# An attention stage whose tile pairs share transposes, with half-sums moved by DMA and operand moves issued a tile later

## The chip, the core and the metric

The kernel runs on one core of a Trainium2 chip. The metric is the device time of one execution in microseconds (us). Engines are named as in the profile: PE is the matmul engine, PEld its weight load, DVE, ACT and POOL the three elementwise engines, SP the engine that issues most of the DMAs.

## The reference

Attention with a bucket mask, then two mixture-of-experts layers on its output. Only the attention stage is changed:

```
q_bits = (einsum('bhsd,dk->bhsk', q, proj) > 0)          # 6 bits give a bucket; k_bits alike
mask   = q_bucket[:, :, :, None] == k_bucket[:, :, None, :]
scores = where(mask, q @ k.T / sqrt(D), -1e9)
scores = scores - max(scores, -1)
attn   = exp(scores);  attn = attn / (sum(attn, -1) + 1e-9)
out    = attn @ v                                         # B=2, H=8, S=768, D=64
x      = out as (1536, 512);  then _moe_ref(x), then _moe2_ref
```

## The kernel before

The 16 heads are worked on as 8 **head pairs** (n). A head pair has 12 **tiles** (t), six for each of its two heads (s), of 128 query rows by 768 keys; 96 tiles in all. A tile's place in its pair is called **r** here (0 to 11). fp32 products are made of a high and a low part (`hi`, `lo`, `ah`, `al`), each of which the PE multiplies at full rate.

A tile goes through these steps, each a function: `qk` (PE: four matmuls into the PSUM tile S, of which there are two), `soft` (DVE: row maximum), `expo` (ACT: exponential and row sum), `inv` (DVE: two small instructions that invert the sum), `norm` (POOL: 128x768 times that inverse), `tr` (PE: six 128x128 transposes into PSUM tiles `tp`, of which there are three), `trh` and `trl` (ACT and DVE: high and low part of the transposed tile, into `ah` and `al`), `av` (PE: matmuls of `ah` and `al` with the V operand `vv` into O). After two tiles, O holds a finished **unit** of 256 query rows: `xa` (ACT) copies it out, and `xp` (POOL, three instructions, only for the second head) adds the two halves and splits the result into the two parts of X, which the expert layer reads.

Beside this, tiles r = 0 to 9 prepare the next head pair in steps `pp`, `pa`, `pd` (function `prep`): r = 0 to 3 transpose raw q and k (`rq`, `rk`), r = 4 and 5 compute the bucket bits (`prep_bits`, six matmuls each), r = 6 to 9 expand them (`prep_hot`). The finished operands are moved by SP's DMAs (`stack`) into the tiles `qa, ka, qb, kb` that `qk` reads. At r = 11 `load` fetches raw q, k and v of the head pair after the next; its `rq` is first read one tile later, at r = 0.

The order of the work is written out by hand: for each tile the loop goes through a table of (step, lag) and calls the step for tile t - lag. There is one table for most tiles, and others for the first and the last head pair, by t's parity. Each engine, and SP's queue too, executes what the loop emits in that order, so that an instruction that waits holds up all that stands behind it on its engine.

After the attention stage comes `_moe_ref`: PE forms the gate's scores from X (lines 476 and 477), weights are fetched in pieces `raw` (three buffers), split by ACT and DVE (lines 427 and 428) into `big`, and PE's first expert products (line 563, `hp`) begin.

Of the kernel before, what the change touches and what calls it, by code (L numbers as in the profile page):

```python
# [39 lines left out]
}  # L40
PREP_V = (3, 3, 6, 9)
# [14 lines left out]
def kernel(ctx, tc, q, k, v, proj, wg1, w1, w2, wg2, w1b, w2b, out):  # L56
    nc = tc.nc
# [224 lines left out]
    def soft(t):  # L282
        w = ap.tile([128, 4], F32, name="w", bufs=6)
        nc.vector.tensor_reduce(w[:, 0:1], Sp[t % 2], op=OP.max, axis=AX.X, negate=True)  # L284
        EN[t] = w

    def expo(t):
        w = EN[t]
        e = ap.tile([128, S], F32, name="e", bufs=2)
        nc.scalar.activation(e, Sp[t % 2], AF.Exp, bias=w[:, 0:1], scale=1.0, accum_out=w[:, 1:2])  # L290
        EN[t] = (e, w)

    def inv(t):
        e, w = EN[t]
        nc.vector.tensor_scalar(w[:, 2:3], w[:, 1:2], 1e-9, None, op0=OP.add)
        nc.vector.reciprocal(w[:, 3:4], w[:, 2:3])  # L296

    def norm(t):
        e, w = EN[t]
        a = ap.tile([128, S], F32, name="a", bufs=3)  # L300
        nc.gpsimd.tensor_tensor(a, e, w[:, 3:4].to_broadcast([128, S]), op=OP.mult)  # L301
        EN[t] = a

    def tr(t, c):
        u, i = divmod(t, 2)
        if i == 0 and c == 0:
            AT[u] = (ap.tile([128, R, 2, 128], F32R, name="ah", bufs=2),
                     ap.tile([128, R, 2, 128], F32R, name="al", bufs=2))
# [5 lines left out]
    def trh(t, c):  # L314
        u, i = divmod(t, 2)
        nc.scalar.activation(AT[u][0][:, 3 * c:3 * c + 3, i, :], TP[t, c], AF.Copy)  # L316

    def trl(t, c):
        u, i = divmod(t, 2)
        ah, al = AT[u]  # L320
        nc.vector.tensor_tensor(al[:, 3 * c:3 * c + 3, i, :], TP[t, c], rd(ah[:, 3 * c:3 * c + 3, i, :]), op=OP.subtract)  # L321


    def av(t):
        u, c = divmod(t, 2)
# [41 lines left out]
    def ahead_v(t):  # L367
# [845 lines left out]
```

## Time and profile before

| | us |
|---|---|
| median of 3 runs (1584.17 to 1585.69) | 1584.64 |
| the profiled execution, its own time | 1586.3 |
| its span in the trace | 1584.6 |
| PE busy in the span | 1553.6 (98%) |
| first score matmul to last one started | 13.64 to 258.04 |

The span is what the trace covers; the profiled execution's time is 1.7 us longer. A matmul's length in the trace covers its whole passage through the array, and matmuls overlap, so the distance from one start to the next is what a matmul costs in a row of them; the same holds, to a smaller degree, of ACT and DVE. "Idle before" in brackets is the time that the engine stood idle ahead of the instruction, with what ended it.

### The profile page before, as it was taken

The numbers are of one execution on the slowest core, as the hardware profiler recorded it, in microseconds if no ns is written. First come the engines' busy times: TensorE is split into PE (matmuls) and PEld (weight loads), VectorE is DVE, ScalarE is ACT, GpSimd is POOL, SyncE is SP. The second block draws the span as 40 slices with busy tenths as digits, with TensorE's granted clock in tenths as the row PEclk, the third lists the DMA queues.
The fourth block names the chain that finished last, engine by engine and source line by source line (L and its number), as shares of the span: only waits on it lengthen the run. The fifth ranks groups of instructions, "written<-read, shape, count | busy, mean of one in ns | idle before, by whom it ended". The sixth has DMA issues, their size and how long they took to land.

```text
span 1584.6 us, 21591 instructions
## 1 busy us (share of the span) xinstructions
PE 1553.6 (98%) x8482; PEld 1309.4 (83%) x8482; DVE 813.0 (51%) x1977; ACT 472.0 (30%) x951; POOL 270.7 (17%) x313
## 2 busy tenths in 40 slices
PE   8999998999999999999999999999999999999998
PEld 6888887788888888888888888888887767888998
DVE  6998897612423324333333332134676377667533
ACT  6998997212200211221221121021121210011343
POOL 4888887020000000000000000000000000111221
PEclk9999999999999999999999999999999999999999
DMA  8665560120200110110120020011000116545531
GB/s 190 147 146 138 121 160 27 42 93 19 77 12 14 67 41 3 64 54 1 38 83 0 14 80 27 1 54 53 1 14 14 41 41 221 190 175 190 190 137 31
DMA packets 83542, 119.13 MB, mean 75 GB/s; under 512 B 43184, under 2 KB 46256, under 8 KB 83440
## 3 DMA queue, kind: packets, MB, share of 16 engines
q1 hardware_dynamic: 75920, 105.15, 22.4%
q0 software_dynamic: 2176, 6.29, 1.3%
q10 hardware_dynamic: 5344, 6.30, 1.1%
q8 instruction: 67, 1.10, 0.3%
q14 instruction: 35, 0.29, 0.1%
HBM read 83.91 MB, written 9.44 MB: 59 GB/s over the span
## 4 chain that ended last, share of the span: by engine, by line
PE 89%; ACT 3%; DVE 3%; DMA 1%; POOL 1%; issue 1%; SPq 1%; POOLq 0%; ACTq 0%; DVEq 0%
PE hp L563 33%; PE yp L582 29%; PE hp L940 5%; PE yp L884 4%; PE tp L311 3%; PE O L331 3%; PE yp L993 3%; PE S L280 2%; PE yp L996 1%; PE sp L1077 1%; PE tp L202 1%; ACT e L290 1%; ACT ah L316 1%; PE yp L998 1%; PE tp L173 1%
## 5 line engine op out<-in xcount | busy, mean ns | idle before, releaser
L563 PE MATMUL hp<-X,big 128*128 128x512 f32 x2304 | 528.9, 390 | 0.0
L563 PEld LDWEIGHTS hp<-X,big 128*128 128x128 f32 x2304 | 431.7, 188 | 89.9
L582 PE MATMUL yp<-big 128*128 128x512 f32 x2016 | 461.2, 389 | 0.0
L582 PEld LDWEIGHTS yp<-big 128*128 128x128 f32 x2016 | 378.2, 188 | 78.4
L564 ACT ACTIVATE big<-hp 128x512 fp32r<-128x512 f32 x176 | 105.2, 598 | 757.5 <-PE hp L563 757.1
L565 DVE SCALAR_TENSOR_TENSOR big<-hp,big 128x512 fp32r<-128x512 f32 x176 | 121.7, 691 | 252.5 <-ACT big L564 252.5
L587 DVE SCALAR_TENSOR_TENSOR acc<-yp,P,acc 128x512 f32<-128x512 f32 x72 | 54.1, 751 | 258.4 <-PE yp L582 258.4
L865 POOL DMA_INDIRECT raw<-x2h,who x4 | 4.1, 1026 | 949.5 <-DVE wg2b L1062 939.0
L301 POOL TENSOR_TENSOR a<-e,w 128x768 f32<-128x768 f32 x96 | 140.8, 1469 | 45.9 <-DVE w L296 26.1
L321 DVE TENSOR_TENSOR al<-tp,ah 128x384 fp32r<-128x384 f32 x192 | 102.8, 547 | 19.1 <-ACT ah L316 18.7
L311 PE MATMUL tp<-ident,a 128*128 128x128 f32 x576 | 94.4, 276 | 8.4 <-ACT hot L233 2.7
L316 ACT ACTIVATE ah<-tp 128x384 fp32r<-128x384 f32 x192 | 91.1, 488 | 16.4 <-PE tp L311 15.9
L940 PE MATMUL hp<-raw,big 128*128 128x192 f32 x488 | 93.7, 338 | 1.2 <-ACT raw L918 1.2
L284 DVE TENSOR_REDUCE w<-S 128x1 f32<-128x768 f32 x96 | 91.1, 949 | 5.1 <-PE S L280 5.1
L311 PEld LDWEIGHTS tp<-ident,a 128*128 128x128 f32 x576 | 67.1, 140 | 24.8 <-issue 5.8
L290 ACT ACTIVATE e<-S,w 128x768 f32<-128x768 f32 x96 | 86.6, 902 | 0.7 <-POOL a L301 0.6
L428 DVE TENSOR_TENSOR big<-raw,big 128x1024 fp32r<-128x1024 f32 x63 | 76.6, 1221 | 14.5 <-ACT big L427 11.1
L940 PEld LDWEIGHTS hp<-raw,big 128*128 128x128 f32 x488 | 79.7, 193 | 2.7 <-ACT raw L918 1.6
L331 PE MATMUL O<-ah,vv 128*128 128x256 f32 x288 | 80.6, 309 | 0.5 <-ACT xm L346 0.5
L427 ACT ACTIVATE big<-raw 128x1024 fp32r<-128x1024 f32 x63 | 64.6, 1053 | 28.1 <-DMA raw<-in_moe_w_dram 26.8
L331 PE MATMUL O<-al,vv 128*128 128x256 f32 x288 | 72.8, 282 | 0.0
L538 DVE SCALAR_TENSOR_TENSOR junk<-acc,wg2b 128x512 bf16<-128x512 f32 x96 | 66.0, 687 | 1.9
(255 smaller groups left out, 1599.6 us busy)
## 6 DMA issues: line engine op xcount, KB each, us to landing
raw<-in_moe_w_dram SPq DMA_DIRECT2D x67, 512.0 KB, 3.5
big<-in_moe_w_dram SPq DMA_DIRECT2D x32, 1024.0 KB, 8.2
qa<-qhi SPq DMA_DIRECT2D x32, 192.0 KB, 3.9
qb<-qlo SPq DMA_DIRECT2D x16, 192.0 KB, 3.8
ka<-khi SPq DMA_DIRECT2D x16, 192.0 KB, 4.3
ka<-klo SPq DMA_DIRECT2D x16, 192.0 KB, 4.0
kb<-khi SPq DMA_DIRECT2D x16, 192.0 KB, 3.7
rv<-in_v_dram SPq DMA_DIRECT2D x16, 192.0 KB, 4.3
```

Of the source, the lines that this page charges most:

```text
L284: nc.vector.tensor_reduce(w[:, 0:1], Sp[t % 2], op=OP.max, axis=AX.X, negate=True)
L290: nc.scalar.activation(e, Sp[t % 2], AF.Exp, bias=w[:, 0:1], scale=1.0, accum_out=w[:, 1:2])
L301: nc.gpsimd.tensor_tensor(a, e, w[:, 3:4].to_broadcast([128, S]), op=OP.mult)
L311: nc.tensor.transpose(p[:, x * 128:x * 128 + 128], EN[t][:, (3 * c + x) * 128:(3 * c + x) * 128 + 128], ident)
L316: nc.scalar.activation(AT[u][0][:, 3 * c:3 * c + 3, i, :], TP[t, c], AF.Copy)
L321: nc.vector.tensor_tensor(al[:, 3 * c:3 * c + 3, i, :], TP[t, c], rd(ah[:, 3 * c:3 * c + 3, i, :]), op=OP.subtract)
L331: nc.tensor.matmul(o, VS[n][:, kt, s].rearrange("p a d -> p (a d)"), a[:, kt].rearrange("p a b -> p (a b)"), start=(kt == 0 and a is ah), ...
L563: nc.tensor.matmul(t, a, b, start=(i == 0), stop=(i == len(prods) - 1))
L564: nc.scalar.activation(hh[:, f], t, AF.Relu)
L565: nc.vector.scalar_tensor_tensor(hl[:, f], t, 0.0, rd(hh[:, f]), op0=OP.max, op1=OP.subtract)
L582: nc.tensor.matmul(t, a, b, start=(i == 0), stop=(i == len(prods) - 1))
L940: nc.tensor.matmul(opened[f], w[:, d, f * 128:f * 128 + 128], xt[:, d], start=(d == 0), stop=(d == HP - 1))
```

## The change

- `PLANS` is now two tables, for even and odd t, in all of the stage. The pipeline is longer: `norm` lags 3 tiles, `tr` 4 to 6, `av` 7 and 8, `xa` 8, `xp` 10.
- Two tiles' 12 transposes fill three `tp` tiles of 512 columns (`tr`, `trh` and `trl` with x = 0, 1, 2), instead of four of 384.
- `inv` handles two tiles' sums in one pair of instructions; `norm` writes in place.
- `vv` has the same layout for both heads. `xa` copies O whole (128x256) in one ACT instruction instead of two of 64x256; the half that has to change partitions is moved by SP's DMAs: one per unit of the first head, two per unit of the second.
- `stack` no longer issues a head pair's moves at once, but appends them to a list; what was in the list when a tile began is issued at the end of that tile (`move(due)`).
- `prep_v` is spread differently (r = 8, 10, 0, 2 instead of 4, 6, 8, 10).

```diff
-        for dst, at, src in moves:
-            nc.sync.dma_start(rd(dst[at:at + 64, s]), rd(src[64 * s:64 * s + 64]))
+        MOVES.extend((dst[at:at + 64, s], src[64 * s:64 * s + 64]) for dst, at, src in moves)
+        if n == 0:
+            move()
...
+    def move(n=None):
+        for dst, src in MOVES[:n]:
+            nc.sync.dma_start(rd(dst), rd(src))
+        del MOVES[:n]
...
+PLANS = ((('tr', 6, 2), ('norm', 3), ('qk', 0), ('av', 8, 1), ('tr', 4, 0), ('pv', 0), ('soft', 0), ('expo', 1), ('th', 6, 2),
+          ('xp', 10), ('tl', 6, 2), ('xa', 8), ('inv', 2), ('th', 4, 0), ('pp', 0), ('pa', 0), ('tl', 4, 0), ('pd', 0)),
+         (('qk', 0), ('av', 7, 0), ('tr', 5, 1), ('norm', 3), ('expo', 1), ('pv', 0), ('th', 5, 1), ('pp', 0), ('soft', 0),
+          ('pa', 0), ('tl', 5, 1), ('pd', 0)))
...
+    def tr(t, x):
         p = aps.tile([128, 512], F32, name="tp", bufs=3)
-        for x in range(3):
-            nc.tensor.transpose(p[:, x * 128:x * 128 + 128], EN[t][:, (3 * c + x) * 128:(3 * c + x) * 128 + 128], ident)
-        TP[t, c] = p[:, :384].rearrange("p (a b) -> p a b", a=3)
+        for y in range(4):
+            i, kt = divmod(4 * x + y, R)
+            nc.tensor.transpose(p[:, y * 128:y * 128 + 128], EN[t + i][:, kt * 128:kt * 128 + 128], ident)
+        TP[t, x] = p
...
     def xa(t):
...
-        nc.scalar.activation(xc[m0:m0 + 64, cs], o[c0:c0 + 64], AF.Copy)
-        nc.scalar.activation(xm[m0:m0 + 64, cs], o[m0:m0 + 64], AF.Copy)
+        if s == 0:
+            xm, xc = XP[n, j] = (ap.tile([128, 256], F32, name="xm", bufs=4), ap.tile([128, 256], F32, name="xc", bufs=4))
+            nc.scalar.activation(xm, o, AF.Copy)
+            nc.sync.dma_start(xc[:D], xm[D:])
+        else:
+            xm, xc = XP[n, j]
+            x1 = x_tile(j)
+            nc.scalar.activation(x1, o, AF.Copy)
+            nc.sync.dma_start(xm[D:], x1[:D])
+            nc.sync.dma_start(xc[D:], x1[D:])
...
-    for t in range(NT + max(lag for _, lag in PLAN)):
-        for nm, lag in plan(t):
+    for t in range(NT + max(x[1] for x in PLANS[0])):
+        due = len(MOVES)
+        for nm, lag, *part in PLANS[t % 2]:
             if 0 <= t - lag < NT:
-                STEPS[nm](t - lag)
+                STEPS[nm](t - lag, *part)
+        if due:
+            move(due)
```

**SP's queue from r = 7 of one head pair to r = 2 of the next.** `hot` is the expanded bucket bits, moved into `qb` and `kb`; `rq, rk, rv` are the raw loads. Before:

```order
L163 DMA qb_121<-hot_905 64x768 x2
L163 DMA kb_122<-hot_981 64x768 x2
L94 DMA rq<-in_q_dram 128x6x64 x2
L94 DMA rk<-in_k_dram 128x6x64 x2
L94 DMA rv<-in_v_dram 128x6x64 x2
L163 DMA qa_115<-qhi 64x768 x2
```

and of the change, where `xc<-xm` is the half of a finished sum of the first head, `x_1096` that of the second:

```order
L347 DMA xc<-xm 64x256
L159 DMA qb_121<-hot_824 64x768 x2
L347 DMA xc<-xm 64x256
L159 DMA kb_122<-hot_894 64x768 x2
L82 DMA rq<-in_q_dram 128x6x64 x2
L82 DMA rk<-in_k_dram 128x6x64 x2
L82 DMA rv<-in_v_dram 128x6x64 x2
L347 DMA xc<-xm 64x256
L352 DMA xm<-x_1096 64x256
L353 DMA xc<-x_1096 64x256
L159 DMA qa_115<-qhi 64x768 x2
```

The move `kb<-hot` and with it the three raw loads now stand behind a DMA that waits for `xa` of tile r = 10.

**PE at r = 0**, where `S_123` is the score tile, and `tp<-ident,rq` the first transposes of the raw q that was loaded at r = 11. Before:

```order
L311 MATMUL tp<-ident,a 128x128 x3
L280 MATMUL S_123<-ka_116,qa_115 128x512
L280 MATMUL S_123<-ka_116,qa_115 128x256
L280 MATMUL S_123<-kb_118,qb_117 128x512
L280 MATMUL S_123<-kb_118,qb_117 128x256
L311 MATMUL tp<-ident,a 128x128 x3
L331 MATMUL O<-ah,vv 128x256
...
L331 MATMUL O<-al,vv 128x256
L173 MATMUL tp<-ident,rq 128x128 x3
```

and of the change:

```order
L309 MATMUL tp<-ident,e 128x128 x4
L277 MATMUL S_123<-ka_116,qa_115 128x512
L277 MATMUL S_123<-ka_116,qa_115 128x256
L277 MATMUL S_123<-kb_118,qb_117 128x512
L277 MATMUL S_123<-kb_118,qb_117 128x256
L331 MATMUL O<-ah,vv 128x256
...
L331 MATMUL O<-al,vv 128x256
L309 MATMUL tp<-ident,e 128x128 x4
L170 MATMUL tp<-ident,rq 128x128 x3
```

The work between the scores and the transposes of `rq` is one group of four transposes more and one group of three less.

**SP's queue at the end of the attention stage.** `wgr` is the gate's weight, `raw` the first pieces of the experts' weights. Before:

```order
L163 DMA kb_118<-hot_3401 64x768 x2
L462 DMA wgr<-in_moe_w_gate_dram 128x4x8
L432 DMA raw<-in_moe_w_dram 128x1024 x4
```

and of the change:

```order
L352 DMA xm<-idle 64x256
L353 DMA xc<-idle 64x256
L352 DMA xm<-pz 64x256
L353 DMA xc<-pz 64x256
L466 DMA wgr<-in_moe_w_gate_dram 128x4x8
L436 DMA raw<-in_moe_w_dram 128x1024 x4
```

All the moves of the sums, the very last unit's too (`pz`), now stand ahead of the expert layer's first loads.

## Rows read from the trace of the kernel before

**Rows 1.** Stretches: length, busy us of PE, PEld, DVE, ACT, POOL, PE clock, DMA share, GB/s.

```profile
13.64:46.59 32.95, 30.17 (x192) 26.83 (x192) 25.74 (x59) 24.78 (x59) 23.21 (x19) 0.90 0.86 195
46.59:77.86 31.27, 30.43 (x224) 27.38 (x222) 27.93 (x68) 28.51 (x70) 26.98 (x25) 1.00 0.62 138
...
108.94:141.32 32.38, 30.77 (x223) 27.43 (x222) 28.67 (x70) 28.90 (x70) 27.61 (x26) 1.00 0.60 137
...
204.05:232.61 28.56, 27.76 (x204) 25.05 (x202) 25.25 (x61) 25.85 (x63) 25.30 (x24) 1.00 0.58 127
232.61:258.04 25.43, 24.19 (x179) 21.94 (x178) 23.34 (x58) 23.35 (x56) 22.29 (x22) 1.00 0.18 62
258.04:278.28 20.24, 17.22 (x108) 11.55 (x107) 14.21 (x26) 12.54 (x25) 10.74 (x13) 1.00 0.21 66
```

**Rows 2.** Timeline of PE in one tile of place r = 5: start, length, instruction.

```profile
152.29 0.60 PE L280 MATMUL S<-ka,qa 128*128 128x512 f32 x2
...
153.08 0.49 PE L311 MATMUL tp<-ident,a 128*128 128x128 f32 x3
153.32 0.37 PE L331 MATMUL O<-ah,vv 128*128 128x256 f32 x1
...
154.12 0.34 PE L202 MATMUL tp<-qhi,pjh 128*128 128x384 f32 x1
...
155.17 0.49 PE L311 MATMUL tp<-ident,a 128*128 128x128 f32 x3
```

**Rows 3.** Timeline of PE, the scores of the first r = 4, and of an r = 10 and the next r = 1.

```profile
23.80 0.60 PE L280 MATMUL S<-ka,qa 128*128 128x512 f32 x2
...
102.19 0.60 PE L280 MATMUL S<-ka,qa 128*128 128x512 f32 x2
...
108.94 0.60 PE L280 MATMUL S<-ka,qa 128*128 128x512 f32 x2
```

**Rows 4.** Timelines of SP and PE around r = 10 to r = 0.

```profile
102.75 1.10 SPq L163 DMA_DIRECT2D kb<-hot  x2
103.89 1.33 SPq L94 DMA_DIRECT2D rq<-in_q_dram  x2
...
140.72 0.52 PE L173 MATMUL tp<-ident,rq 128*128 128x128 f32 x3 [0.47 <-DMA rq<-in_q_dram]
```

**Rows 5.** DMAs issued between 40 and 262 us: count, size, median us to landing.

```profile
kb<-hot SPq DMA_DIRECT2D x14, 192.0 KB, 2.8
rq<-in_q_dram SPq DMA_DIRECT2D x12, 192.0 KB, 3.6
```

**Rows 6.** Timeline of ACT, the two copies of a unit's sums.

```profile
157.51 0.38 ACT L345 ACTIVATE xc<-O 64x256 f32<-64x256 f32 x1
157.91 0.38 ACT L346 ACTIVATE xm<-O 64x256 f32<-64x256 f32 x1
```

**Rows 7.** Timeline of the end of the attention stage, several engines.

```profile
231.39 41.54 SPq L432 DMA_DIRECT2D raw<-in_moe_w_dram  x4
...
267.89 0.28 PE L331 MATMUL O<-al,vv 128*128 128x256 f32 x1
268.21 0.38 ACT L345 ACTIVATE xc<-O 64x256 f32<-64x256 f32 x1 [1.54 <-PE O L331]
...
271.35 1.22 DVE L428 TENSOR_TENSOR big<-raw,big 128x1024 fp32r<-128x1024 f32 x1 [3.43 <-POOL X L360]
...
275.96 1.06 ACT L427 ACTIVATE big<-raw 128x1024 fp32r<-128x1024 f32 x1 [4.01 <-DMA raw<-in_moe_w_dram]
277.05 1.23 DVE L428 TENSOR_TENSOR big<-raw,big 128x1024 fp32r<-128x1024 f32 x1 [0.42 <-ACT big L427]
```

**Rows 8.** DMA issues of the page: count, size, us to landing.

```profile
raw<-in_moe_w_dram SPq DMA_DIRECT2D x67, 512.0 KB, 3.5
```

**Rows 9.** The view of rows 1 for two stretches early in the kernel.

```profile
10.00:14.00 4.00, 1.14 (x5) 0.59 (x4) 1.46 (x3) 3.13 (x6) 0.00 (x0) 1.00 0.95 199
14.00:21.00 7.00, 6.19 (x24) 5.24 (x23) 4.16 (x8) 2.86 (x6) 1.47 (x1) 0.51 0.97 224
```

More of the change, by code (lines that the diff above doesn't have):

```diff
@@ L294, in inv @@
         e, w = EN[t]
-        nc.vector.tensor_scalar(w[:, 2:3], w[:, 1:2], 1e-9, None, op0=OP.add)
-        nc.vector.reciprocal(w[:, 3:4], w[:, 2:3])
+        nc.vector.tensor_scalar(w[:, 2], w[:, 1], 1e-9, None, op0=OP.add)
+        nc.vector.reciprocal(w[:, 3], w[:, 2])
     def norm(t):
         e, w = EN[t]
[L300 to L308, printed above, removed]
-        p = aps.tile([128, 512], F32, name="tp", bufs=3)
-        for x in range(3):
-            nc.tensor.transpose(p[:, x * 128:x * 128 + 128], EN[t][:, (3 * c + x) * 128:(3 * c + x) * 128 + 128], ident)
-        TP[t, c] = p[:, :384].rearrange("p (a b) -> p a b", a=3)
@@ L314, in trh @@
[L314 to L325, printed above, removed]
+        i = t % 2
+        nc.gpsimd.tensor_tensor(e, e, w[:, 3, i:i + 1].to_broadcast([128, S]), op=OP.mult)
+        EN[t] = e
@@ new lines, in tr, with trh @@
+    def tr(t, x):
+        p = aps.tile([128, 512], F32, name="tp", bufs=3)
+        for y in range(4):
+            i, kt = divmod(4 * x + y, R)
+            nc.tensor.transpose(p[:, y * 128:y * 128 + 128], EN[t + i][:, kt * 128:kt * 128 + 128], ident)
+        TP[t, x] = p
+    def trh(t, x):
+        if x == 0:
+            AT[t // 2] = (ap.tile([128, 2, R, 128], F32R, name="ah", bufs=2),
+                          ap.tile([128, 2, R, 128], F32R, name="al", bufs=2))
+        ah = AT[t // 2][0].rearrange("p i a b -> p (i a b)")[:, 512 * x:512 * x + 512]
+        nc.scalar.activation(ah, TP[t, x], AF.Copy)
@@ L326, in av, with trl @@
+    def trl(t, x):
+        ah, al = (y.rearrange("p i a b -> p (i a b)")[:, 512 * x:512 * x + 512] for y in AT[t // 2])
+        nc.vector.tensor_tensor(al, TP[t, x], rd(ah), op=OP.subtract)
+    def av(t, c):
+        u = t // 2
         n, s, j = unit(u)
-        o = Op[:, u % 2]
+        o = Op[:, u % 2].rearrange("p (i b) -> p i b", i=2)
         ah, al = AT[u]
@@ L330, in av, with x_tile @@
             for a in (ah, al):
-                nc.tensor.matmul(o, VS[n][:, kt, s].rearrange("p a d -> p (a d)"), a[:, kt].rearrange("p a b -> p (a b)"),
+                nc.tensor.matmul(o, VS[n][:, kt, s].rearrange("p a d -> p (a d)"), a[:, :, kt],
                                  start=(kt == 0 and a is ah), stop=(kt == R - 1 and a is al))
+    def x_tile(j):
+        if j % 3 == 1:
+            return ap.tile([128, 512], BF, name="idle").bitcast(F32)
+        return ap.tile([128, 256], F32, name="pz" if j % 3 else "x1")
@@ L360, in xp @@
-        nc.gpsimd.tensor_tensor(xl, xm[:, cs], rd(xh), op=OP.subtract)
+        nc.gpsimd.tensor_tensor(xm, xm, xc, op=OP.add)
+        nc.gpsimd.tensor_tensor(xh, xm, zero.to_broadcast([128, 256]), op=OP.add)
+        nc.gpsimd.tensor_tensor(xl, xm, rd(xh), op=OP.subtract)
     def ahead(t, part):
@@ L371, in ahead_v @@
                 prep_v(0, i)
-        if r % 2 == 0 and r >= 4 and n + 1 < NP:
-            prep_v(n + 1, r // 2 - 2)
+        if r in (8, 10) and n + 1 < NP:
+            prep_v(n + 1, r // 2 - 4)
+        if r in (0, 2) and 0 < n < NP:
+            prep_v(n, r // 2 + 2)
         if r == TU - 1 and n + 2 < NP:
             load(n + 2)
-    STEPS = dict(qk=qk, soft=soft, expo=expo, inv=inv, norm=norm, tr0=lambda t: tr(t, 0), tr1=lambda t: tr(t, 1),
-                 th0=lambda t: trh(t, 0), th1=lambda t: trh(t, 1), tl0=lambda t: trl(t, 0), tl1=lambda t: trl(t, 1),
-                 av=av, xa=xa, xp=xp, pp=lambda t: ahead(t, 0), pa=lambda t: ahead(t, 1), pd=lambda t: ahead(t, 2),
+    STEPS = dict(qk=qk, soft=soft, expo=expo, inv=inv, norm=norm, tr=tr, th=trh, tl=trl, av=av, xa=xa, xp=xp, pp=lambda t: ahead(t, 0), pa=lambda t: ahead(t, 1), pd=lambda t: ahead(t, 2),
                  pv=ahead_v)
@@ L389 @@
     held, HELD = HELD, None
-    def plan(t):
-        seg = 0 if t < TU else 3 if t >= NT else 2 if t >= NT - TU else 1
-        return PLANS.get((seg, t % 2), PLAN)
     for x in held:
```

44 lines of the change are left out of this document (16 added, 28 removed), and 11 rows, old and new, of the table PLANS.

## The prediction

> **What bounds the kernel now.** I read three views in this order: busy time by stretch, the timeline of PE inside a tile, and the timeline of SP between two head pairs. The stretches [rows 1] are cut where a tile r = 1 starts its scores. A head pair lasts 31.27 us in the first full stretch; over the five from 46.59 to 204.05 the mean is (204.05 - 46.59) / 5 = 31.49. In such a stretch PE, ACT, DVE and POOL are all busy for 26.98 to 30.43 us: no engine has much room, and a wait on one spreads to the others.
>
> PE's own need is smaller than its busy time says, since matmuls overlap. Distances between starts give it [rows 2]: the scores of a tile cost 153.08 - 152.29 = 0.79, three transposes 0.24 (0.08 each), half of a unit's `av` 0.80, the six bit matmuls 1.05 (0.18 for one). A tile costs 0.79 + 0.80 + 6 x 0.08 = 2.07 without preparation; twelve cost 24.84, and the preparation of the next pair adds 4 x 0.24 + 2 x 1.05 + 4 x 0.18 = 3.78. So PE needs 28.6 of the 31.49: 2.9 us per pair are waits on the mean, 2.5 in a pair such as that from 77.86 to 108.94 (31.08), and nothing that lightens ACT, DVE or POOL can give back more than these.
>
> Where they lie: from the scores of r = 10 to those of the next r = 1 the pair takes 108.94 - 102.19 = 6.75 us [rows 3], against 4.14 + 2.31 = 6.45 of PE's need. The rest lies in r = 1 to 9, which take 31.08 - 6.75 = 24.3 against 9 x 2.07 + 3 x 0.24 + 2 x 1.05 + 4 x 0.18 = 22.2, and where ACT and DVE have the preparation to do as well.
>
> **What the change saves.** Per pair of tiles ACT issues one copy of O instead of two, which start 157.91 - 157.51 = 0.40 apart [rows 6], and three high parts instead of four of the same columns in all; DVE saves an `inv` and a fixed cost. With ACT 28.5 of 31.27 busy and six units in a pair, 6 x 0.40 = 2.4 us less on ACT is as much as r = 1 to 9 wait. PE's own work does not change (as many transposes, the same matmuls); four of these nine tiles now have eight transposes and five have four, which makes it 22.0. So I let r = 1 to 9 fall to 22.0 plus a rest. The rest I take from POOL: its work stays (26.98 a pair [rows 1]), and `xp` now waits for DMAs that stand behind six operand moves on SP. At 0.55 per issue (1.10 for two [rows 4]) these take 3.3, the landing at least 2.8 [rows 5], and `xp` follows `xa` by two tiles, about 4.6: some 1.5 us late once or twice a pair, most of it inside the slack of `norm`. I take 0.6 per pair, between nothing (slack covers all) and 1.8 (PE waits for the whole delay).
>
> **What the change adds at r = 10 to r = 0.** This is the term on which most rests. Before, `kb<-hot` is issued 0.56 after the scores of r = 10 and the raw q 1.14 later, the second half of it at about 103.89 + 0.65 = 104.54, 2.35 after those scores [rows 3, 4]. With a landing of 3.6 [rows 5] it is there at 5.95, just ahead of PE's need: where it was late, PE stood 0.47 for it [rows 4].
>
> Now both stand behind `xc<-xm`, which waits for the copy of O at r = 10. Count from the start of that tile: four transposes 0.32, scores 0.79, `av` 0.80, so `av` ends at 1.91; ACT starts about 0.2 after such an end (268.21 [rows 7], the last matmul having started at 267.89 and costing 0.80 / 6 = 0.13) and takes 0.38: SP goes on at about 2.6. Then one move of 0.5, two of `kb` 1.15, the first raw q 0.65: the second raw q is issued at about 5.0 and lands at 8.6. PE gets to its transposes at 4.14 (tiles 10 and 11) + 0.32 + 0.79 + 0.80 + 0.32 = 6.4. It stands 2.2 us, 1.0 of them already in the scores, which need `kb` (issued at 3.1, landed at 5.9, needed at 4.9). With 0.24 for the transposes, r = 10 to r = 1 takes 8.9 instead of 6.75. While PE stands the others catch up, which is why I add nothing for them here. Bounds: a landing of 2.8 as of `kb` gives a stand of 1.4, and one 1.1 longer, as in the stretch of 32.38 [rows 1], 3.3.
>
> The Trainium skill (DMA: Bandwidth & Descriptors, Anatomy of one DMA) says that any semaphore wait of a DMA happens on the issuing sequencer before dispatch, which speaks against putting moves behind a copy that is not done. The trace agrees: four `raw` issues of SP form one row of 41.54 us [rows 7], whose last issue waits. By this rule the stand is the 2.2 us above; if a waiting DMA let the others pass, it would be none.
>
> **What it adds at the end.** Before, the first pieces of the experts' weights are issued from 231.39 on [rows 7], during the attention stage, and wait in their buffers; the last `av` matmul starts at 267.89, 9.85 after the last tile's scores at 258.04; `xp` ends by 271.35; the fourth piece is split at 277.05 + 1.23 = 278.28, the end of my last stretch of 20.24 us [rows 1]. After, counted from the last scores: the drain has the same chain for the last two tiles, but POOL does two norms in a row before the last transposes; I put the last `av` at 10.3. Copy done at 11.0, two moves until 12.1, the gate's weight until 12.7, then the pieces. Each is 512 KB: the first lands 3.5 later [rows 8], the others every 2.3 (512 KB at 224 GB/s [rows 9]): 16.3, 18.6, 20.9. ACT's split takes 1.06 and DVE's 1.23 [rows 7], so the first buffer is free at 18.6 and the fourth piece, behind the third, lands at 23.2 and is split at 25.7 with a copy or so on DVE before it. That is 25.7 - 20.24 = 5.5 late. PE has nothing else to do there, and after it the expert layer is bound by PE. Bounds: 4.0 if the three pieces come at once with the first, 7.0 if the drain is 1.5 longer.
>
> **The sum**, by the stretches of rows 1:
> - Start to 46.59: the first tiles have neither transposes nor `av` of lag 7, so r = 4 to 9 run at PE's need with less of it. Up to the scores of r = 4 at 23.80 [rows 3] nothing changes; from there, by the costs of rows 2, I come to r = 10 at 36.6 and with 8.9 to 45.5: -1.1 (-2 to 0).
> - Five pairs: 8.9 + 22.0 + 0.6 = 31.5 against 31.1, a pair without late raw loads (the late ones I take as equally frequent): +0.4 each, +2.0 (0.6 x 5 less with no rest: -1.0; 1.8: +8.0).
> - 204.05 to 232.61: 22.0 + 0.6 + 4.14 = 26.7 against 28.56, as no raw loads are left: -1.8 (-2.4 to -0.6).
> - The last pair, 25.43: no preparation, PE's need 11 x 2.07 = 22.8, a stand of 1.0 for `kb`; but POOL has 22.29 there already and comes late by about as much as the rest: 0 (-1.5 to +1).
> - The end: +5.5 (4.0 to 7.0).
>
> Sum +4.6: from 1586.3 for the profiled execution to 1590.9. The median is 1.7 below the profiled execution: **1589.2 us**.
>
> **Rivals.**
> - *The raw loads do not hold PE* (faster). If PE reaches r = 0 late anyway, or SP gets past the copy 2.2 us sooner, a pair is 22.0 + 0.6 + 6.7 = 29.3: -1.8 instead of +0.4, five times, so 11 less and with the start's 2 as well some 1578. It decides from a stand below about 0.6 on. For it: PE had 0.2 to spare before, and landings differ. Against: the queue's order is fixed, and SP's wait for ACT is real. 0.12.
> - *Nothing much comes of it* (same): r = 1 to 9 falls to 22.1 and gives 2.2 back where the stand takes 2.2, the end costs 4.0. Then -1.1 - 0.5 - 2.3 + 0 + 4.0 = +0.1: 1585. 0.22.
> - *POOL becomes the bound* (slower): every delay of `xp` reaches `norm` and PE's transposes, rest 1.8. Then -1.1 + 8.0 - 0.6 + 1.0 + 5.5 = +12.8: 1597. For it: POOL has 26.98 of 31.27 and gains nothing. Against: `norm` has a tile more of lag than before. 0.16.
> - *PE's clock falls at the end* (slower). Early in the kernel the granted clock was 0.51, the lower level of 1.2 GHz, in a stretch that followed one with PE busy 1.14 of 4.00 us [rows 9]. At the end PE would now stand about 5 us and work with gaps for 9 more. If the first 6 us of expert products ran at half clock, 3 us more: 1592. 0.12. The Trainium skill (TensorE: Matmul & The Clock Gate, Part 1) says that throttled is the default state and that activity releases it; by that rule, too, 1592.
>
> My forecast as summed has 0.38. A difference of 0.2% (3.2 us) is about what a measurement of this kernel can tell from none. Faster by more: the first rival, 0.12. Within: the second and a part of my own where the landing is short, 0.22 + 0.08 = 0.30. Slower: the rest, 0.58. The range, 1582 to 1597, leaves out the first rival and the far end of the third.
>
> **What the profile after should show.** At r = 0, PE idle before the second score pair with `kb<-hot`, and before the transposes of `rq` with the raw load, 2.2 us together; SP's waits led by ACT's copies of O; r = 1 to 9 in 22 to 23 us with ACT below 27 a pair; the first `raw` issue after the last copy, and ACT's first split waiting for its landing. I am wrong if PE does not stand at r = 0, if the pieces of weights are there when ACT gets to them, or if POOL's `xp` waits for its moves so long that `norm` ends most of PE's waits.

## The result, and the profile after

The changed kernel takes 1593.09 us (median of 6 runs, 1591.39 to 1596.62); the kernel before, run beside it, 1585.16 (6 runs, 1583.86 to 1587.27). The ratio is 1.0051, with a 95% interval of 1.0037 to 1.0064: 0.5% slower. The forecast was 1589.2, with a range of 1582 to 1597. The profiled execution took 1593.4 (span 1591.7), against 1586.3 (1584.6) before, 7.1 more.

The stretches of the kernel after, cut at the same starts of scores as [rows 1], and with its columns; the last one ends, as there, when the fourth piece of weights is split:

```profile
13.65:45.63 31.98, 26.45 (x171) 23.76 (x172) 25.03 (x44) 23.37 (x50) 20.77 (x18) 0.95 0.88 199
45.63:77.12 31.49, 29.64 (x223) 27.88 (x222) 27.13 (x49) 26.10 (x56) 26.91 (x26) 1.00 0.70 157
...
204.59:231.41 26.82, 26.82 (x206) 25.81 (x205) 23.18 (x42) 23.10 (x51) 22.87 (x22) 1.00 0.64 143
231.41:257.19 25.78, 23.29 (x178) 21.61 (x176) 24.19 (x41) 21.19 (x45) 24.17 (x23) 1.00 0.16 37
257.19:283.84 26.65, 20.68 (x128) 14.36 (x126) 15.03 (x24) 12.46 (x21) 13.12 (x15) 0.94 0.43 130
```

Against [rows 1], the start is 0.97 shorter (31.98 for 32.95), the five pairs take 204.59 - 45.63 = 158.96 against 157.46 (+1.50), the next stretch is 1.74 shorter, the last pair 0.35 longer, and the end 26.65 against 20.24 (+6.41). That is +5.55. ACT has become lighter as meant, 26.10 a pair against 28.51, and the pair is no shorter. After the end the two kernels differ by another 1.5; that goes with PE's clock, as the last section shows.

Where the lighter ACT's gain went is seen on PE between an r = 10 and the next r = 1. In the timeline of PE, these are the starts of the scores of r = 10 (100.02), r = 0 (104.42) and r = 1 (108.94), with PE's stands between them:

```profile
100.02 0.60 PE L277 MATMUL S<-ka,qa 128*128 128x512 f32 x2
...
104.42 0.59 PE L277 MATMUL S<-ka,qa 128*128 128x512 f32 x2
105.88 0.59 PE L277 MATMUL S<-kb,qb 128*128 128x512 f32 x2 [0.86 <-DMA kb<-hot]
108.66 0.52 PE L170 MATMUL tp<-ident,rq 128*128 128x128 f32 x3 [1.04 <-DMA rq<-in_q_dram]
108.94 0.59 PE L277 MATMUL S<-ka,qa 128*128 128x512 f32 x2
```

And SP's queue in the same time:

```profile
102.33 0.46 SPq L347 DMA_DIRECT2D xc<-xm  x1
102.83 1.23 SPq L159 DMA_DIRECT2D kb<-hot  x2
104.11 1.34 SPq L82 DMA_DIRECT2D rq<-in_q_dram  x2
```

SP issues the move of the sum at 102.33, 2.31 after the scores of r = 10, because it waits for ACT's copy; `kb<-hot` and raw q follow it, and PE stands for each in turn. From r = 10 to r = 1 the pair takes 108.94 - 100.02 = 8.92 here, against 6.75 in [rows 3]. The waits of SP's queue and of PE between 40 and 262 us (us in total, times, longest):

```profile
SPq L347 <- ACT xm L346: 40.7, 15, 4.5
...
PE S L277 <- DMA kb<-hot: 5.3, 6, 1.2
PE tp L170 <- DMA rq<-in_q_dram: 4.8, 4, 1.7
```

The end, which answers to [rows 7]: SP's issues, and then ACT's and DVE's first work on the weights, PE's first gate matmul and first expert product, and POOL's last instruction on the sums.

```profile
270.51 0.59 SPq L353 DMA_DIRECT2D xc<-pz  x1
271.14 0.59 SPq L466 DMA_DIRECT2D wgr<-in_moe_w_gate_dram  x1
271.78 6.75 SPq L436 DMA_DIRECT2D raw<-in_moe_w_dram  x4
...
273.80 0.40 PE L480 MATMUL sp<-X,wgs 128*16 128x512 f32 x1 [4.29 <-DVE wgs L469]
274.29 0.73 POOL L365 TENSOR_TENSOR X<-xm,X 128x256 fp32r<-128x256 f32 x1
275.80 1.06 ACT L431 ACTIVATE big<-raw 128x1024 fp32r<-128x1024 f32 x1 [5.87 <-DMA raw<-in_moe_w_dram]
276.94 1.23 DVE L432 TENSOR_TENSOR big<-raw,big 128x1024 fp32r<-128x1024 f32 x1 [3.20 <-ACT big L431]
...
280.93 0.40 PE L567 MATMUL hp<-X,big 128*128 128x512 f32 x1
```

The pieces of weights are issued at 271.78, behind the last sum's moves, 40 us later than in [rows 7], and ACT and DVE wait for them. PE does not: between 257 and 305 us its waits have none for `big`. What PE stands for, 4.29 us, is the gate's weight `wgr`, issued at 271.14 behind the same moves; the first expert product follows the 24 gate matmuls without a gap.

### The profile page after: what moved, and what is told of

Read it like the earlier page. It is cut to its first block, busy times and chain, and to the rows that moved or that the text cites. A ratio compares the mean times of both kernels' runs of the same rounds, so it can differ in the third digit from the quotient of the medians.

```text
span 1591.7 us, 21428 instructions
## 1 busy us (share of the span) xinstructions
PE 1548.0 (97%) x8482; PEld 1311.2 (82%) x8482; DVE 809.2 (51%) x1833; ACT 453.2 (28%) x855; POOL 269.9 (17%) x313
## 4 chain that ended last, share of the span: by engine, by line
PE 85%; DMA 4%; ACT 3%; DVE 2%; SPq 2%; POOL 2%; issue 1%; POOLq 0%; ACTq 0%; DVEq 0%
PE hp L567 32%; PE yp L586 29%; PE hp L944 5%; PE yp L888 4%; PE yp L997 3%; PE S L277 2%; PE O L331 2%; PE tp L309 2%; PE yp L1000 1%; PE sp L1081 1%; ACT e L289 1%; DMA rq<-in_q_dram 1%; SPq L159 1%; PE tp L199 1%; DMA raw<-in_moe_w_dram 1%
## 5 line engine op out<-in xcount | busy, mean ns | idle before, releaser
L301 POOL TENSOR_TENSOR e<-e,w 128x768 f32<-128x768 f32 x96 | 138.9, 1468 | 42.7 <-DVE w L296 27.5
L321 DVE TENSOR_TENSOR al<-tp,ah 128x512 fp32r<-128x512 f32 x144 | 98.2, 683 | 15.8 <-ACT ah L317 13.3
L317 ACT ACTIVATE ah<-tp 128x512 fp32r<-128x512 f32 x144 | 86.2, 600 | 25.2 <-PE tp L309 22.2
L309 PE MATMUL tp<-ident,e 128*128 128x128 f32 x576 | 84.6, 274 | 2.2 <-POOL e L301 2.1
L331 PE MATMUL O<-ah,vv 128*128 128x256 f32 x288 | 72.9, 283 | 1.3 <-ACT xm L346 0.8
L309 PEld LDWEIGHTS tp<-ident,e 128*128 128x128 f32 x576 | 66.5, 141 | 4.8 <-POOL e L301 3.7
```

The source lines that it names most:

```text
L301: nc.gpsimd.tensor_tensor(e, e, w[:, 3, i:i + 1].to_broadcast([128, S]), op=OP.mult)
L309: nc.tensor.transpose(p[:, y * 128:y * 128 + 128], EN[t + i][:, kt * 128:kt * 128 + 128], ident)
L317: nc.scalar.activation(ah, TP[t, x], AF.Copy)
L321: nc.vector.tensor_tensor(al, TP[t, x], rd(ah), op=OP.subtract)
```

## The experiments

All are edits of the kernel after. The table has four distances taken from the starts of instructions in each trace: **hold**, from the scores of r = 10 to those of the next r = 1, mean of six; **body**, from r = 1 to r = 10, mean of six; **last**, the first distance ahead of the last pair; **end**, from the last tile's scores to the first expert product `hp`. Ratios are to the kernel before, run beside each.

| run | median us | ratio (95%) | hold | body | last | end |
|---|---|---|---|---|---|---|
| before | | | 7.16 | 24.26 | 6.67 | 17.04 |
| after | 1593.09 | 1.0051 (1.0037 to 1.0064) | 9.01 | 22.73 | 7.36 | 23.74 |
| e1 moves at once | 1598.02 | 1.0075 (1.0058 to 1.0092) | 7.76 | 24.65 | 7.32 | 23.65 |
| e2 loads early | 1606.70 | 1.0130 (1.0113 to 1.0147) | 10.72 | 23.26 | 7.38 | 23.71 |
| e3 loads, hot early | 1602.46 | 1.0103 (1.0086 to 1.0120) | 9.75 | 23.38 | 5.99 | 24.17 |
| e4 last on ACT's queue | 1599.83 | 1.0085 (1.0068 to 1.0101) | 9.03 | 22.71 | 7.35 | 27.27 |
| e5 hot, q early | 1582.42 | 0.9970 (0.9960 to 0.9980) | 7.07 | 22.85 | 6.57 | 23.61 |
| e6 sums by ACT | 1581.66 | 0.9973 (0.9964 to 0.9983) | 7.20 | 23.44 | 6.41 | 20.50 |
| e7 last sums by ACT | 1591.34 | 1.0034 (1.0025 to 1.0044) | 8.96 | 22.81 | 7.36 | 20.38 |
| e8 is e5 and e7 | 1578.91 | 0.9961 (0.9945 to 0.9978) | 7.10 | 22.84 | 6.15 | 20.37 |
| e9 hot early | 1585.92 | 0.9999 (0.9989 to 1.0008) | 7.77 | 22.69 | 6.21 | 24.90 |
| e10 q early | 1587.43 | 1.0004 (0.9993 to 1.0015) | 7.98 | 22.79 | 7.37 | 23.71 |
| e11 r = 10 by ACT | 1578.16 | 0.9949 (0.9936 to 0.9963) | 7.14 | 22.80 | 6.27 | 20.37 |
| e12 is e11, single inverses | 1576.33 | 0.9936 (0.9922 to 0.9949) | 7.05 | 22.86 | 6.27 | 21.15 |

### Four edits that put things earlier on SP's queue, or on another queue

My first theory was that lateness as such costs: what is issued sooner lands sooner. e1 issues every operand move at once:

```diff
-        if n == 0:
-            move()
+        move()
```

> Only the late issue of the operand moves is undone. Theory (SP's order holds PE at r = 0): the move of kb no longer stands behind the copy of O at r = 10, and the raw q comes 1.2 us sooner (two moves of 0.55 are no longer between), so PE stands about 1.0 instead of 2.1 at r = 0: from r = 10 to the next r = 1 about 7.7 us instead of 8.8, six times 1.1 and 1.0 in the last pair less, 1593 - 7.6 = 1585.5. Rival (the moves of q and k, now ahead of the halves of the sums on SP, make POOL's xp late): r = 1 to 9 grows by about as much, 1590 to 1594, with POOL's waits on the moves above the 4.8 us that they total now between 40 and 262 us.

The hold falls to 7.76, but the body rises by 1.92 on the mean. (It is 26.99 in one pair, in which PE also ran at half clock from 66.6 to 70.0, and 23.86 to 24.61 in the others, 1.45 more than in the kernel after.) Two groups of waits, PE's and POOL's, say why:

```profile
PE tp L308 <- POOL e L300: 15.0, 14, 2.8
...
POOL xm L362 <- DMA xc<-x: 13.4, 5, 3.4
```

The operand moves now stand ahead of the halves of the sums, POOL's add waits for these, its norms stand behind that add, and PE's transposes behind the norms. The rival was right in kind: the late moves of q and k protect POOL. In size it was not, as 1598.02 lies above its 1590 to 1594.

e2 puts the six raw loads at r = 8 instead of r = 11, and e3 adds the moves of `hot` at once:

```diff
-        if r == TU - 1 and n + 2 < NP:
+        if r == 8 and n + 2 < NP:
             load(n + 2)
...
                     stack(n, s, ((dst, 64, hot),))
+                move()          (e3 only)
```

> Only the raw loads are issued earlier, at r = 8 instead of r = 11, ahead of the two copies that SP waits for. Theory: the wait for raw q at r = 0 goes, the wait for kb (about 1.0 to 1.2 us) stays, r = 10 to r = 1 takes about 7.7 us: six times 1.1 less, 1586.5. Rival (PE stands at r = 0 because ACT, DVE or POOL are behind after r = 9, and the raw load only ends the wait last): no change beyond 2 us, 1591 to 1593, with another releaser in its place.

> The raw loads at r = 8 as in the run before, and the moves of the bucket bits (hot) at once, so that nothing that PE needs at r = 0 stands behind a copy. Theory: PE's stand at r = 0 is gone, r = 10 to r = 1 takes 6.6 to 6.9 us, r = 1 to 9 stays at 22.7: six times 2.1 and about 1.0 in the last pair less, 1579.5, faster than the kernel before by 0.35%. Rival (without the stand POOL, with 27 us of work per pair, or DVE does not catch up): r = 1 to 9 grows by 0.5 to 1.5, 1582 to 1589.

Both are slower than any rival said, and the hold grows, to 10.72 and 9.75. In e2 PE's waits are all for one move (between 40 and 262 us):

```profile
PE S L277 <- DMA kb<-hot: 18.5, 7, 4.0
```

The median landing of that move, between 40 and 240 us:

```profile
kb<-hot SPq DMA_DIRECT2D x12, 192.0 KB, 4.1
```

And the timeline of SP around an r = 10 whose scores start at 105.16, with PE's scores of r = 0, which stand for `kb`, and the clock behind that stand, in the columns of [rows 1]:

```profile
101.38 1.29 SPq L82 DMA_DIRECT2D rq<-in_q_dram  x2
...
105.61 1.28 SPq L82 DMA_DIRECT2D rv<-in_v_dram  x2
...
109.55 1.24 SPq L159 DMA_DIRECT2D kb<-hot  x2
...
113.63 1.01 PE L277 MATMUL S<-kb,qb 128*128 128x512 f32 x2 [3.48 <-DMA kb<-hot]
```

```profile
113.20:116.60 3.40, 2.97 (x13) 2.87 (x14) 1.80 (x4) 0.38 (x1) 0.00 (x0) 0.50 0.01 3
```

The loads take SP from 101.38 to 106.89, and what stands behind them goes out late: `kb<-hot` 4.39 after the scores of r = 10 here, and 2.92 to 4.39 in the six pairs, where it was 2.81 to 2.94 in the kernel after. It also lands in 4.1, where it took 3.0 there. In e3 `kb<-hot` no longer stands behind the copy of r = 10, but it stands behind the loads, and goes out 2.56 to 4.66 after those scores; only ahead of the last pair, where no loads are left, does it go out at 0.76, and there the distance is 5.99 instead of 7.36. So the price of `kb` was shown there, and where to put the loads was not.

Part of the growth is the clock's. After the stand shown PE is at half clock (two matmuls take 1.01 where they took 0.59). The one hold of e2 that is at full clock takes 9.17, with a stand of 2.34; three with stands of 2.43 to 2.64 and 3.4 us at half clock take 10.30 to 10.60. In e3 the two holds at full clock take 8.64 and 8.56, less than in the kernel after, and the other four 9.58 to 11.19.

e4 issues the last pair's sum moves from ACT's queue:

```diff
-            nc.sync.dma_start(xc[:D], xm[D:])
+            (nc.scalar if n == NP - 1 else nc.sync).dma_start(xc[:D], xm[D:])
...
-            nc.sync.dma_start(xm[D:], x1[:D])
-            nc.sync.dma_start(xc[D:], x1[D:])
+            q = nc.scalar if n == NP - 1 else nc.sync
+            q.dma_start(xm[D:], x1[:D])
+            q.dma_start(xc[D:], x1[D:])
```

> Only in the last head pair the half-sums are moved by ACT's DMA queue instead of SP's, so that the first loads of the expert layer stand behind no copy of that pair. Theory: the first pieces are there when ACT gets to them, the first split waits for the last xp instead; the fourth piece is split about 4.5 us sooner after the last scores (about 22 instead of 26.7): 1588.5. Rival (the end is late because of the longer drain and the last xp, not of the loads): at most 1.5 us less, 1591.5 to 1593.

The end became 3.5 longer. (The profiled execution took 1594.89, at a mean granted clock of 0.992; the other three, 1599.8 to 1599.9, had 0.987 to 0.988, so a part of the median's loss goes with the clock.) SP, the ACT queue, and what waits for them:

```profile
264.17 17.07 SPq L437 DMA_DIRECT2D raw<-in_moe_w_dram  x4
268.80 0.61 ACTq L354 DMA_DIRECT2D xc<-idle  x1
...
275.23 0.73 POOL L364 TENSOR_TENSOR xm<-xm,xc 128x256 f32<-128x256 f32 x1 [4.66 <-DMA xc<-idle]
...
279.66 1.23 DVE L433 TENSOR_TENSOR big<-raw,big 128x1024 fp32r<-128x1024 f32 x1 [10.38 <-POOL X L366]
```

The pieces do go out 7.6 sooner (8.1, counted from the last scores), but then they are ahead of the sums on the DMA engines: the move issued at 268.80 holds POOL until 275.23, and DVE's first split waits for POOL's last add. The Trainium skill (DMA: Bandwidth & Descriptors, Issuing engines are not separate DMA queues) says that transfers share the same engines whoever issues them, and that issuing elsewhere only saves the sequencer's time; this trace agrees, as the 6.4 us of that 64 KB move show (1.9 to 3.6 for such moves in the kernel after). My theory of the end fell: what holds DVE there is the last `xp`, not only the place of the loads in SP's queue. PE was at half clock for 6.8 us of this end, 3.4 in the kernel after, so the 3.5 are not the moves' alone.

### Taking the wait away

e5 issues the moves of `hot` at once and raw q alone at r = 10, ahead of that tile's sum; k and v stay. e6 moves no sum by DMA, and e7 only not those of the last pair; e8 is e5 and e7.

```diff
+        if r == 10 and n + 2 < NP:          (e5, e8, e10)
+            load(n + 2, "q")
         if r == TU - 1 and n + 2 < NP:
-            load(n + 2)
+            load(n + 2, "kv")
...
                     stack(n, s, ((dst, 64, hot),))
+                move()                       (e5, e8, e9)
...
         if s == 0:
-            xm, xc = XP[n, j] = (...)
+            XP[n, j] = (...)
+        if COND:      (e6: True; e7, e8: n == NP - 1; e11, e12: that or (s, j) == (0, 1))
+            m = slice(64 * s, 64 * s + 64)
+            for x, h in zip(XP[n, j], (o[:D], o[D:])):
+                nc.scalar.activation(x[m], h, AF.Copy)
+        elif s == 0:
+            xm, xc = XP[n, j]
             nc.scalar.activation(xm, o, AF.Copy)
```

> The moves of the expanded bits are issued at once (r = 7 and 9) and raw q at r = 10, ahead of the move of that tile's sum; raw k and v stay at r = 11. Theory (the hold at r = 0 is the order of SP's queue behind a waiting move): kb<-hot lands before r = 11 needs it and raw q before r = 0's transposes, the step r = 0 to r = 1 falls from 4.4 to 2.4 us in six pairs and from 3.2 to 1.9 in the last, 13 us less: 1580 us (1577 to 1583). Rival 1 (whatever is ahead of the sums' moves makes POOL late, as when the loads stood at r = 8): r = 0 falls but r = 1 or 2 grows by as much, 1588 or more. Rival 2 (raw q lands late whatever its place, since k and v share the DMA engines): r = 0 stays over 3.5, 1587 to 1590.

> No sum is moved by DMA: each unit's O is copied by two ACT instructions of 64x256, as before the change; all else as after. Theory (SP's wait for the copy is what costs): r = 0 falls by 2 us in six pairs and 1.0 in the last, the end by 4, and ACT's 0.40 per unit gives back half of 2.4 us per pair in r = 1 to 9: 1593 - 13 - 4 + 8 = 1584 us (1580 to 1588). Rival (the saved copy is worth its full time, 2.4 us per pair in eight pairs = 19): 1595 or more.

> Only the last head pair's sums are copied by ACT in two instructions instead of moved by DMA. Theory (the end is late by the moves of the last sum, two issues and a landing, and by raw pieces behind them): xp ends about 2.5 us sooner, the pieces are issued 3 to 7 us sooner, and the first expert products start 3 to 4 us sooner: 1589.5 us (1588 to 1591). Rival (the longer drain of the new pipeline sets the end, POOL's norms and the last av): at most 1 us gained, 1592 to 1594.

> Both edits together: moves of expanded bits at once with raw q at r = 10, and the last pair's sums by ACT. If the two holds are independent places, the gains add: 13 + 3.5 us less than after, 1576.5 us (1573 to 1580), 0.5% faster than the kernel before. If either falls, it is the other alone.

e5: the hold falls from 9.01 to 7.07, below that of before, and the body stays. In time that is 1.0051 - 0.9970 = 0.81%, 12.8 us, where 13 was expected. (The scores that first need the new `kb` are those of r = 0, not of r = 11.) The same place in its trace, the timelines of PE

```profile
99.52 0.60 PE L278 MATMUL S<-ka,qa 128*128 128x512 f32 x2
...
106.06 0.52 PE L170 MATMUL tp<-ident,rq 128*128 128x128 f32 x3 [0.19 <-DMA rq<-in_q_dram]
106.33 0.60 PE L278 MATMUL S<-ka,qa 128*128 128x512 f32 x2
```

and of SP:

```profile
100.28 1.11 SPq L159 DMA_DIRECT2D kb<-hot  x2
101.44 1.33 SPq L82 DMA_DIRECT2D rq<-in_q_dram  x2
102.88 0.58 SPq L348 DMA_DIRECT2D xc<-xm  x1
```

Raw q goes out 1.92 after the scores of r = 10 instead of 4.09, and the sum's move 3.36 after them instead of 2.31, which POOL bears: PE's waits for POOL's norms between 40 and 262 us are 2.0 in all, 2.1 in the kernel after.

e6: with no sum on SP the hold is 7.20 and the end 20.50, and ACT pays for it with 0.59 in the body (23.44 against 22.85 of e5). Over the five pairs, e6 takes 152.68 and e5 149.26, so copying O whole is worth 3.42 / 5 = 0.68 us a pair, of the 2.4 us that ACT is spared (0.65 against e11, which keeps the order of the kernel after and copies one unit of six twice). 1584 was expected, from half of the 2.4.

e7: the end falls from 23.74 to 20.38, 3.4 less, where 3.5 was expected; the ratios give 0.17%, 2.7 us (its median of 1591.34 is just above the expected range, but so was the kernel before that ran beside it, 1586.42 for 1585.16). e8: 0.9961, 14.3 us below after, where the two apart give 12.8 + 2.7 = 15.5: the gains nearly add.

### One half each, and the wait alone

> Only the moves of the expanded bits are issued at once; raw q, k and v stay at r = 11, behind the move that waits for the copy of O. Theory (two holds of about 1 us each, kb<-hot ahead of the scores and raw q ahead of its transposes, both from SP's order): the first is gone, and raw q is issued two issues (1.15 us) sooner but still late; the step r = 0 to r = 1 falls from 4.5 to about 3.3 us, and to 1.9 in the last pair, 8.5 us less than after: 1584.5 us (1583 to 1587). Rival (raw q's landing sets r = 0 by itself, the hold of kb only hides in it): 1590 or more.

> Only raw q is issued earlier, at r = 10 ahead of the sum's move; the moves of the expanded bits stay a tile late, behind it. Theory: the hold of raw q goes, that of kb<-hot stays: r = 0 falls from 4.5 to about 3.4 us in six pairs, the last pair stays at 3.2, 6.5 us less than after: 1586.5 us (1584.5 to 1588.5). Rival (kb<-hot now lands later beside raw q, and takes back what raw q gives): 1590 or more.

> The order of SP's queue stays as after (bits a tile late, loads at r = 11). Only the unit whose copy falls on r = 10 and the units of the last pair are copied by ACT in two instructions; no move of a sum stands ahead of kb<-hot and raw q at r = 10 any more. Theory (that one waiting move is the whole hold): r = 0 falls from 4.5 to 2.4 us in six pairs and to 1.9 in the last, the end by 3; ACT's 0.40 once per pair costs nothing to 0.4: 1579 us (1577 to 1582), as with both orders changed. Rival (a move a tile late and the loads at r = 11 are themselves too late, whoever copies): r = 0 stays above 3.5, 1586 or more.

Each half of e5 takes away the stand that it names and leaves the other. Around the same r = 10, first e9, with the scores of r = 10 at 100.29, then e10, with them at 99.83, in which `kb` is the late one:

```profile
107.61 0.52 PE L170 MATMUL tp<-ident,rq 128*128 128x128 f32 x3 [1.08 <-DMA rq<-in_q_dram]
```

```profile
105.72 0.59 PE L277 MATMUL S<-kb,qb 128*128 128x512 f32 x2 [0.90 <-DMA kb<-hot]
```

The hold falls by 1.24 in e9 and by 1.03 in e10, and by 1.94 in e5: two stands of about 1 us, one behind the other.

e11 leaves SP's order as in the kernel after, `kb<-hot` a tile late and the loads at r = 11. It only takes away what SP waits for, by letting ACT make two copies of the one unit that falls on r = 10 (and of the last pair's). SP's queue around an r = 10 that starts at 97.99:

```profile
98.75 1.10 SPq L159 DMA_DIRECT2D kb<-hot  x2
99.90 1.34 SPq L82 DMA_DIRECT2D rq<-in_q_dram  x2
...
104.87 0.51 SPq L353 DMA_DIRECT2D xc<-xm  x1
```

`kb<-hot` is issued 0.76 after the scores of r = 10, raw q at 1.91, and the hold is 7.14. So the order was not the fault by itself, nor the tile of delay: it was the one move in that order that waits for a copy not yet made. (Its own issue takes SP 0.46, and `kb<-hot` goes out 2.05 sooner; in e5 the move is still there, behind the two, and the hold is gone as well.) e11 runs at 0.9949 of before.

### What is left of the end

The end of e7, e8 and e11 is still 3.3 longer than before. Taken apart on PE, from starts in each trace: from the last scores to the last `av` matmul, from there to the first gate matmul, from there to the first `hp`:

| run | last `av` | to the gate | to `hp` |
|---|---|---|---|
| before | 9.85 | 0.12 | 7.07 |
| after | 12.04 | 4.57 | 7.13 |
| e7 | 13.20 | 0.11 | 7.07 |
| e11 | 13.18 | 0.12 | 7.07 |
| e12 | 13.97 | 0.11 | 7.06 |

So e7 took away the wait for the gate's weight, 4.5, and paid 1.2 in the drain, where PE now waits 2.5 for ACT's copies of O, for 1.3 in the kernel after. What is left is the drain alone: these 1.2, and 2.2 that the kernel after has too. e12, made from e11, inverts each sum of the last pair by itself (`inv1` stands in the tables at lag 1) and does its norm a tile sooner; `inv` and the late norm skip that pair:

```diff
+    def inv1(t):
+        if t >= LAST:
+            e, w = EN[t]
+            i = slice(t % 2, t % 2 + 1)
+            nc.vector.tensor_scalar(w[:, 2, i], w[:, 1, i], 1e-9, None, op0=OP.add)
+            nc.vector.reciprocal(w[:, 3, i], w[:, 2, i])
```

> The copies by ACT at r = 10 and in the last pair stay as in the run before; in the last pair each tile's sum is inverted by itself right after its exponential, and its norm goes one tile sooner. Theory (what is left of the longer end, 3.3 us, is that two sums wait for each other, so that POOL begins the last two norms 5.4 us after the last scores instead of 2.9): the last norms begin about 2 us sooner, the last matmuls on V and the last split with them, and the first expert products start 18.4 us after the last scores instead of 20.4: 1576 us (1575 to 1577.5). Rival (POOL is busy with the norms ahead of them, or PE waits for ACT's two copies of O, and these set the drain): the expert products move by less than 0.7 us, 1578 us.

The time came as expected, 1576.33, and not in the way expected: the end did not shorten (21.15 against 20.37), the last pair did, from r = 1 to its last scores (21.18 against 22.96). POOL in e11, then in e12, around the last scores (246.98 and 244.24):

```profile
248.33 2.89 POOL L301 TENSOR_TENSOR e<-e,w 128x768 f32<-128x768 f32 x2 [0.40 <-DVE w L296]
252.36 2.90 POOL L301 TENSOR_TENSOR e<-e,w 128x768 f32<-128x768 f32 x2 [1.13 <-DVE w L296]
```

```profile
245.28 7.18 POOL L320 TENSOR_TENSOR e<-e,w 128x768 f32<-128x768 f32 x5
```

The waits of 0.40 and 1.13 for the inverses are gone, PE reaches the last scores sooner, and then five norms stand in a row on POOL and end 252.46 - 244.24 = 8.2 after them, as in e11 (255.26 - 246.98 = 8.3). In the kernel before the last two norms ended 5.8 after (at 263.82, the scores at 258.04). The joint inverse with its late norm costs 1.8 us in the last pair (22.96 to 21.18), of which 0.8 comes back in the end; so the two distances explain 1.0 of the 1.8 between the medians of e11 and e12, whose intervals overlap. What stands ahead of the drain in e12 is POOL's row of norms, and a way to shorten that was not tried.

## Why the prediction was right, point by point

- **The hold at r = 10 to r = 0**: predicted 8.9 for 6.75, made of a stand for `kb` of 1.0 and one for raw q of 1.2. Measured 9.01 on the mean of six, 0.86 and 1.04 in the pair shown, and the hold falls by 1.24 when `kb` is taken away (e9) and by 1.03 when raw q is (e10). The rule that I weighed (the Trainium skill, DMA: Bandwidth & Descriptors, Anatomy of one DMA: a wait is served on the issuing sequencer) holds in e11: with the wait gone and the order kept, the hold is gone. The rival that raw loads do not hold PE is out. That the number came so near is in part luck: 7.14 are left in e11, so the wait costs 1.87 on top of 7.14, where I had 2.2 on top of 6.75. And my count begins 0.32 ahead of the scores of r = 10, with that tile's four transposes; counted from the scores it gives 8.5, not 8.9.
- **r = 1 to 9**: predicted 22.6; measured 22.73. PE's need of 22.0 and a rest of 0.7 hold. Of the 1.53 gained on the 24.26 of before, e6 shows 0.82 without any saved copy (24.26 to 23.44): ACT's copy, which I named first, is the smaller part. What the rest of 0.7 consists of was not taken apart. I had put it on POOL; PE's waits for POOL's norms come to 2.1 us between 40 and 262, 0.3 a pair, so that its size came out is in part luck.
- **The start** (-1.1) came to -0.97, **the five pairs** (+2.0) to +1.50, **204.05 to 232.61** (-1.8) to -1.74, **the last pair** (0) to +0.35. The stand of 1.0 for `kb` ahead of the last pair is shown by e5 and e9: 7.36 falls to 6.57 and 6.21.
- **The end** (+5.5) came to +6.41 by the split of the fourth piece, and to +6.70 by PE's first `hp`. A term was mis-sized: "I put the last `av` at 10.3" after the last scores; it starts at 269.23, 12.04 after. The chain behind it was as laid out, about 2 us later: pieces issued 14.6 after the last scores for 12.7, ACT's first split 18.6 for 16.3. Then pieces came faster than every 2.3 us, which left 0.9. But PE came to be late by another path than mine. I let it wait for the pieces; it has no wait for them, and stands for the gate's weight behind the same moves. Of the 6.70, the longer drain is 2.19 and the way from the last `av` to the gate 4.45. The size came near because the same moves stand ahead of both. In e4 the pieces went out sooner, and the end got longer. Without the last moves (e7) 3.4 come back, and 3.3 stay, all of them in the drain.
- **POOL as the bound** did not come: its own waits for the moves are 4.8 us in all. e1 shows how near it is, 1.92 a pair with the moves of q and k ahead of the sums (1.45 without the pair at half clock).
- **The clock at the end**: it did fall there, to 0.51 for 3.4 us (last section), and the gate matmuls, not the expert products, ran at half speed. What it cost can be estimated: e9 has 6.8 us of it there (0.50) and an end of 24.90, e5 and e10 have 3.4 and ends of 23.61 and 23.71, so another 3.4 us at half clock are worth some 1.2, not the 3 of the rival. In the kernel after it hardly shows: from the first gate matmul to `hp` it takes 7.13, and e7, with full clock there but a wait of 1.3 for DVE among the gate matmuls, 7.07.

The sum was +4.6 and the profile shows +7.1: 0.9 more from the end, next to nothing from the other terms together (+0.13, -0.50, +0.06, +0.35), and 1.5 that comes late in the kernel. The medians differ by 7.9, since the median of the kernel after lies 0.3 below its profiled execution, where I took 1.7.

## What to carry to other kernels

A DMA that waits for an engine blocks every later DMA of its queue, so ask of each moved or added transfer what stands behind it and when PE needs that; here one 64 KB move in the wrong tile cost 12 us and hid a gain of 9 (1.53 in each of six bodies). Bringing transfers forward is not the remedy by itself: what is put ahead delays something else (the sums behind operands in e1, the operands behind loads in e2 and e3, where a longer stand also brought the clock down), and the cure was to take the one wait away (e11), or to let only the urgent transfer pass it (e5). A saving on an engine that is 91% busy was worth little more than a quarter of its length (0.68 of 2.4).

## What the runs showed of the hardware

PE's granted clock falls for stretches whose place and length differ between kernels that have the same work there. Three stretches of about the same point of the expert layers, in the columns of [rows 1]: before, after, and e12.

```profile
1372.00:1380.00 8.00, 7.42 (x40) 6.27 (x40) 1.98 (x7) 1.81 (x5) 1.96 (x3) 0.57 0.93 275
```

```profile
1376.80:1387.00 10.20, 8.45 (x39) 6.82 (x40) 1.98 (x7) 1.81 (x5) 1.95 (x3) 0.50 0.73 227
```

```profile
1360.50:1374.20 13.70, 12.97 (x60) 10.86 (x61) 4.16 (x16) 2.48 (x7) 1.96 (x3) 0.50 0.89 302
```

PE is at 1.2 GHz here for 6.8 (the first row reaches past it on both sides), 10.2 and 13.7 us. From the 151st expert product (`hp` and `yp` counted together) to the end, the same work takes 1268.8, 1270.5 and 1271.5; in the seven profiles with 6.8 us it is 1268.5 to 1269.6 (1270.4 in e1), in the four with 10.2 it is 1270.5 to 1271.1, in the three with 13.7 it is 1271.5 to 1272.6. The last 1.5 of the profile's +7.1 lies there, and no step of the change reaches so far. Why one execution gets the longer stretch was not tried. The clock moves whole executions too: of 27 of the kernel before, run beside e5 to e8, the twelve with a mean granted clock of 0.993 take 1586.8 in the median, the nine with 0.995 take 1584.7. Differences of 2 us between medians, as from e11 to e12, are no larger than that.

The same happens in the first pair: e5 has the instructions of the kernel after there, and yet PE runs at half clock from 22.40 to 29.20, behind a stretch in which it was busy 1.42 of 3.40 us, where it had been busy 1.98 in the kernel after; from the first scores to the second pair's r = 1 e5 takes 33.20, the kernel after 31.98. The rows of after, then of e5:

```profile
19.00:22.40 3.40, 1.98 (x13) 1.37 (x11) 1.73 (x5) 1.34 (x4) 1.37 (x1) 1.00 0.97 212
22.40:29.20 6.80, 5.63 (x36) 5.35 (x37) 6.49 (x11) 5.42 (x13) 6.13 (x6) 1.00 1.07 238
```

```profile
19.00:22.40 3.40, 1.42 (x10) 1.09 (x9) 1.20 (x3) 0.12 (x1) 1.47 (x1) 1.00 1.08 212
22.40:29.20 6.80, 5.50 (x18) 5.11 (x19) 4.34 (x8) 4.10 (x9) 5.70 (x5) 0.50 1.12 232
```

At the end of attention in the kernel after, where PE had stood 4.29 us, the gate matmuls ran at half clock:

```profile
274.30:277.70 3.40, 3.40 (x10) 1.11 (x9) 0.76 (x1) 1.53 (x2) 0.87 (x2) 0.51 0.96 348
```
